# Before the first unit: only batch 0's odd half folded, on VectorE; its even half added up by DMAs during the first tile

## The chip, the cores and the metric

One core of one Trainium2 chip runs the whole program. The metric is the device time of one execution in microseconds; the time of a kernel is the median of its runs. Engines are called by the names of the profile: PE (TensorE), DVE (VectorE), ACT (ScalarE), POOL (GpSimd), and SP, the queue that issues most DMAs.

## The reference

```python
X = np.fft.fft(x, axis=1)            # x is (4, 3072, 256), float32
X = np.fft.fft(X, axis=2)
x = X.real.reshape(B * S, D)
h = x @ w_in                         # 256 -> 2048
x = np.maximum(0.01 * h, h) @ w_out  # 2048 -> 256
xk = mu_k * x + (1 - mu_k) * x_prev  # x_prev: one token earlier
xr = mu_r * x + (1 - mu_r) * x_prev
k = np.maximum(xk @ w_k, 0)          # 256 -> 1024
return sigmoid(xr @ w_r) * (k * k @ w_v)
```

Everything is float32, and the weights arrive as 64-bit floats.

## The kernel before

The real part of a Fourier transform over the sequence is a cosine transform of one mixture of the rows and a sine transform of another. Four rows of x (s, M-s, N-s, M+s, with N = 3072 and M = 1536) enter only through sums and differences; making these is the *fold*. Folded rows come in 6 groups of 128 per batch and give four classes: Pe and Qe (even frequencies; P cosine, Q sine) and Po and Qo (odd ones). A class is two PE products, `fft_a` with the first three groups and a first table, `fft_b` with the last three and a second table; ACT and DVE turn their results into a row of 768 values (`classes`). Tables a, b, a2, b2 serve the even classes, c, d, c2, d2 the odd ones. The transform over the 256 features is moved into the weights: `w_in_mm(q)` multiplies eighth q of w_in by a cosine and a sine table, `w_in_split` writes the result as two float32r parts, `w_in_row` takes one more small product from it. Weights are converted from 64-bit floats by ACT, DVE and POOL in steps (`w_in_parts`, and for w_out the three steps `wout[q][0..2]`): POOL makes the part `r`, for which PE's product or DVE's last step waits.

Feature 128 is its own column and is transformed apart: `c_fold` folds it, `c_a` and `c_b` multiply it (4 columns, one per batch), and its result goes to DRAM (`cd_o`, `cd_e`) and comes back broadcast as `cb`, which each unit adds.

After that each batch has three tiles of 512 columns, and a tile 16 *units* of 128 of the 2048 hidden features. In `step`, PE computes the P half of the next unit (`mm_a`, L548), the Q half of this one (`mm_b`, L560) and, two units later, the product with w_out (`outmm`, L571). DVE and ACT do `ev`, `g`, the leaky function and the split into `gh` and `gl`. `mm_b` adds onto the accumulator that DVE's `ev` has read, so PE waits for `ev`. In the first tile `boot(u)` also prepares the rest of w_in and w_out, and a loop table (`pe_u`, `qe_u`) says after which unit Pe and Qe of the batch are computed; beside it the next batch is folded by accumulating DMAs that POOL issues (`second`). The last 40% of the time is the second network.

The order on each engine is the order of the program text (the kernel is scheduled by hand), so an instruction that waits holds up all behind it on its engine. Before the first unit the text runs from L457 to the definition of `boot`. For batch 0 the fold (`full`) makes even and odd halves together, six DVE or POOL operations per group: groups 0, 1, 3 and 4 on DVE, 2 and 5 on POOL. Batch 0's four classes are float32 products (two PE passes each); later batches split into float32r parts (`fft_src`), nine one-pass products in place of three.

Of the kernel before, what the change touches and what calls it, by code (L numbers as in the profile page):

```python
# [78 lines left out]
def fft_mlp_kernel(ctx, tc, xa, xb, x7, x8, x87, tb, tbs, alt, ce, so, mu, w_in, w_out, w_k, w_v, w_r, out):  # L79
# [117 lines left out]
    def fold_ops(b):  # L197
        st, eo, o7s = {}, {}, []
        pm = fft.tile([P, 6, 2, 2, P], F32, tag="pm", bufs=1, name=f"pm{b}")
        if b == 0:  # L200
            plus, minus = pm[:, 0:3], pm[:, 3:6]
            plus, minus = (t.rearrange("p g i o n -> p (g i) o n") for t in (plus, minus))
            folded[b] = {"Pe": plus[:, :, 0], "Qe": minus[:, :, 1], "Po": minus[:, :, 0], "Qo": plus[:, :, 1]}
        else:
            for g in range(6):
                eo[g] = pm[:, g]
            folded[b] = pm, o7s

        def first(g, p=None):
            if b == 0:  # L210
                tag, bufs = ("yo", 2) if p is work else ("xl", 4)
                t = st[g] = p.tile([P, 2, 2, D], F32, tag=tag, bufs=bufs, name=f"xl{b}_{g}")
                Q.dma_start(t[:, 0], xa[b, g])
                Q.dma_start(t[:, 1], xb[b, g, :, :, 0:D])
            else:
                st[g] = fft.tile([P, 2, D], F32, tag="xl", bufs=2, name=f"xl{b}_{g}")
                Q.dma_start(eo[g][:, 0], xa[b, g, :, :, 0:P])
                Q.dma_start(st[g], xa[b, g])


        def second(g):
            E = eo[g][:, 0]
            G.dma_start(E, xa[b, g, :, :, P:D], accum_op=ALU.add)
            G.dma_start(st[g], xb[b, g, :, :, P:P + D], accum_op=ALU.add)
            G.dma_start(E, xb[b, g, :, :, 0:P], accum_op=ALU.add)
            G.dma_start(E, xb[b, g, :, :, P:D], accum_op=ALU.add)


        def full(g, E, tags):
            t = st[g].rearrange("p z o d -> p (z o) d")  # L230
            home = {"gh": mv, "gl": mv, "Qh": mv}
            e, o, eo[g] = (home.get(tag, work).tile([P, 4, P], F32, tag=tag, bufs=2, name=f"f{n}{g}")
                           for n, (tag, _) in zip("eoc", tags))
            eo[g] = eo[g].rearrange("p (z o) n -> p z o n", z=2)
            E.tensor_tensor(e, t[:, :, :P], t[:, :, P:], op=ALU.add)
            E.tensor_tensor(o, t[:, :, :P], t[:, :, P:], op=ALU.subtract)
            E.tensor_tensor(eo[g][:, 0], e[:, 0:2], e[:, 2:4], op=ALU.add)
            E.tensor_tensor(eo[g][:, 1], o[:, 0:2], o[:, 2:4], op=ALU.subtract)
            fin(g, 2, E)
            fin(g, 3, E)  # L240

        def fin(g, q, E=V):
            if q == 1:
                E.tensor_tensor(eo[g][:, 1], st[g][:, :, :P], st[g][:, :, P:], op=ALU.subtract)
            elif q == 2:
                E.tensor_tensor(plus[:, g], eo[g][:, :, 0], eo[g][:, :, 1], op=ALU.add)
            else:
                E.tensor_tensor(minus[:, g], eo[g][:, :, 0], eo[g][:, :, 1], op=ALU.subtract)
# [5 lines left out]
        def fold7(E=V):  # L254
# [6 lines left out]
            if b == 0:  # L261
                E.tensor_tensor(plus[0:1, 0, 1], o7[:, 0], o7[:, 1], op=ALU.subtract)
            else:
                o7s.append(o7)

        return first, second, full, fin, load7, fold7
# [8 lines left out]
    def fft_src(b, kind, h):  # L275
        pm, o7s = folded[b]
        i = 0 if kind[0] == "P" else 1
# [3 lines left out]
        s = pm[:, 3 * h:3 * h + 3, i]  # L281
        V.tensor_tensor(t, s[:, :, 0], s[:, :, 1], op=ALU.add if kind in ("Pe", "Qo") else ALU.subtract)
# [5 lines left out]
    def fft_mm(b, kind, h, ps, stop):  # L288
        t = tabs[KINDS[kind][h]]
        how = dict(skip_group_check=True) if h else {}  # L290
        if b == 0:
            src = folded[b][kind]
            terms = [(src[:, 3 * h + c], t[:, c]) for c in range(3)]
# [113 lines left out]
    def w_out_load(q, ahead=False):  # L407
        if q < 8:
            st = load_f64(w_out[q * 256:(q + 1) * 256].rearrange("(k p) d -> p k d", p=P), 2, D, ahead)
            s = slice(2 * q % HF, 2 * q % HF + 2)  # L410
            wout[q] = f64_hi_lo(uoh[2 * q // HF][:, s], uol[2 * q // HF][:, s], st, 2, D, *((mv, "gl") if q < 3 else (stage, "f")))


    def c_fold():
        c8 = mv.tile([P, 6, 2, 4], F32, tag="gh", bufs=2, name="c8")
        V.tensor_tensor(c8, x8t[:, :, 0:2], x8t[:, :, 2:4], op=ALU.add)
        V.tensor_tensor(c8p, c8[:, :, 0], c8[:, :, 1], op=ALU.add)
        V.tensor_tensor(c8m, c8[:, :, 0], c8[:, :, 1], op=ALU.subtract)
        V.memset(c87, 0.0)
        V.tensor_tensor(c87[0:1], x87t[:, 0], x87t[:, 1], op=ALU.add)  # L420

    def c_a(src, t0, extra):
        ps = ps_s.tile([P, 512], F32, tag="s", name="cps")
        for c in range(3):
            T.matmul(ps[:4, :JP], src[:, c], tabs[t0][:, c], start=(c == 0), stop=(c == 2 and not extra))
        if extra:
            T.matmul(ps[:4, :JP], c87, altt, start=False, stop=True)
        ev = work.tile([4, JP], F32, tag="fv", bufs=2, name="cev")
# [15 lines left out]
    pairs = [TORD[i:i + 2] for i in range(0, 8, 2)]  # L444
    later_tabs = 3 * TORD

    def next_pair():
        load_pair_tab(*pairs.pop(0))
# [52 lines left out]
    w_in_split(1)  # L501
    wout[0][0]()
    po = fft_a(0, "Po")
    ca = c_a(c8m, "c", False)
    w_in_row(1)
    w_in_parts(2)
    fft_b(0, "Po", *po)
    wout[0][1]()
    cs0 = c_b(c8m, "d", "o", *ca, "g")
    cur_c = load_c(0, 0)  # L510
    wout[1][0]()
    qo = fft_a(0, "Qo")
    wout[0][2]()
    next_pair()
    w_in_parts(3)
    wout[1][1]()
    fft_b(0, "Qo", *qo)
    next_pair()
    cur = split_tile(0, 0, "P") + split_tile(0, 0, "Q")
    w_in_mm(2)  # L520
# [260 lines left out]
    w_in_split(2)  # L781
    wout[1][2]()
    for b in range(B):

        pe_u, qe_u, f0, f1 = (2, 10, 13, 36) if b == 0 else (1, 4, 10, 36)
        po_u, qo_u = 37, 40
        done = 0
        for ti in range(NT):
# [3 lines left out]
            for u in range(NF):  # L792
# [292 lines left out]
```

## Time and profile before

| | |
|---|---|
| median of 3 runs (lowest to highest) | 1510.63 us (1509.85 to 1511.0) |
| the profiled execution's own time | 1511.04 us |
| its span in the trace | 1509.3 us |
| mean granted PE clock | 0.994 |
| PE busy in the span | 1479.3 us (98%) |
| DVE busy | 1032.8 us (68%) |
| ACT busy | 890.5 us (59%) |
| POOL busy | 168.2 us (11%) |

The span runs from the first to the last instruction; the execution's own time holds 1.74 us more around it. Times in rows count from the span's start. "Idle before" in brackets is how long an engine did nothing before that row, and what ended it.

### The profile page before, as it was taken

To read this page: it belongs to the slowest core of one execution; us is meant where nothing else is said; L and a number is where in the kernel's file an instruction comes from. 1 tells how busy PE (TensorE), PEld (TensorE's weight loads), DVE (VectorE), ACT (ScalarE), POOL (GpSimd) and SP (SyncE) were. 2 spreads that over 40 slices of the span, in tenths; PEclk is the share of its full clock that TensorE was granted. 3 is DMA by queue.
4 is the path that set the end of the run, shared out by engine and by line. 5 is a ranking of instruction groups with operands and counts; after the bars stand their busy time and mean duration, and the time that the engine had idled before them with its cause. 6 is when DMAs were issued, how large, how long until landed. Compare 5 with 4: busy or idle time off the path is not lost.

```text
span 1509.3 us, 17754 instructions
## 1 busy us (share of the span) xinstructions
PE 1479.3 (98%) x6506; PEld 1212.3 (80%) x6506; DVE 1032.8 (68%) x1426; ACT 890.5 (59%) x1469; POOL 168.2 (11%) x165
## 2 busy tenths in 40 slices
PE   5899999999999999999999999999999999999998
PEld 3677888888888888888888887888888888888887
DVE  8776667676767766666667775766667676766665
ACT  2565566656566656566566665656555656565554
POOL 4333401023101142010001000000000000000000
PEclk8999999999999999999999999999999999999999
DMA  7434723276213464132411102221212121211200
GB/s 252 140 95 110 119 56 129 85 195 103 35 67 123 164 123 92 14 122 99 137 43 36 56 1 84 84 71 56 71 56 84 43 84 44 83 63 63 70 29 28
DMA packets 97810, 128.71 MB, mean 85 GB/s; under 512 B 29190, under 2 KB 64775, under 8 KB 94650
## 3 DMA queue, kind: packets, MB, share of 16 engines
q1 hardware_dynamic: 74618, 87.29, 18.0%
q0 software_dynamic: 23104, 40.29, 11.7%
q8 instruction: 51, 0.84, 0.2%
q14 instruction: 37, 0.30, 0.1%
HBM read 99.67 MB, written 27.88 MB: 85 GB/s over the span
## 4 chain that ended last, share of the span: by engine, by line
PE 95%; DVE 1%; DMA 1%; ACT 0%; issue 0%; POOL 0%; ACTq 0%; DVEq 0%
PE o L571 34%; PE v L927 17%; PE kps L884 17%; PE ps L560 9%; PE ps L548 9%; PE rps L935 4%; PE wps L383 1%; PE dps L592 0%; DMA pm<-in_xa 0%; DMA xl<-in_xb 0%; PE cps L434 0%; PE f0Qe L299 0%; PE f0Pe L299 0%; PE f1Qe L299 0%; PE f2Qe L299 0%; DMA y<-yo 0%
## 5 line engine op out<-in xcount | busy, mean ns | idle before, releaser
L637 DVE SCALAR_TENSOR_TENSOR g<-ev,ps 128x512 f32<-128x512 f32 x192 | 131.7, 686 | 194.5 <-PE ps L560 194.4
L888 ACT ACTIVATE rl<-kps 128x512 f32<-128x512 f32 x190 | 113.9, 599 | 230.4 <-PE kps L884 227.0
L619 DVE TENSOR_TENSOR gl<-g,gh 128x1024 fp32r<-128x1024 f32 x192 | 239.5, 1248 | 1.4 <-ACT gh L104 1.4
L889 DVE SCALAR_TENSOR_TENSOR k<-kps,rl 128x512 f32<-128x512 f32 x190 | 131.6, 693 | 148.4 <-ACT rl L888 147.7
L104 ACT ACTIVATE gh<-g 128x1024 fp32r<-128x1024 f32 x192 | 202.8, 1056 | 51.1 <-PE o L571 50.0
L107 ACT ACTIVATE g<-ps 128x512 f32<-128x512 f32 x192 | 114.9, 598 | 163.6 <-DVE g L637 162.2
L571 PE MATMUL o<-gh,uoh 128*128 128x512 f32 x768 | 211.3, 389 | 0.0
L571 PE MATMUL o<-gh,uol 128*128 128x512 f32 x768 | 211.1, 389 | 0.0
L571 PE MATMUL o<-gl,uoh 128*128 128x512 f32 x768 | 211.1, 389 | 0.0
L571 PEld LDWEIGHTS o<-gh,uoh 128*128 128x128 f32 x768 | 144.2, 188 | 30.4
L571 PEld LDWEIGHTS o<-gl,uoh 128*128 128x128 f32 x768 | 144.2, 188 | 30.0
L571 PEld LDWEIGHTS o<-gh,uol 128*128 128x128 f32 x768 | 144.2, 188 | 29.9
L553 DVE SCALAR_TENSOR_TENSOR ev<-cb,w,ps 128x512 f32<-128x512 f32 x192 | 143.4, 747 | 2.6 <-PE ps L548 0.8
L111 DVE TENSOR_TENSOR k2l<-k,k2h 128x512 fp32r<-128x512 f32 x190 | 129.6, 682 | 0.5 <-ACT k2h L104 0.5
L927 PE MATMUL v<-k2h,wvh 128*128 128x512 f32 x382 | 121.7, 389 | 0.1
L927 PE MATMUL v<-k2l,wvh 128*128 128x512 f32 x382 | 121.5, 389 | 0.0
L927 PE MATMUL v<-k2h,wvl 128*128 128x512 f32 x382 | 121.5, 389 | 0.0
L107 ACT ACTIVATE g<-g 128x512 f32<-128x512 f32 x192 | 119.6, 623 | 0.0
L884 PE MATMUL kps<-mh,wkh 128*128 128x512 f32 x380 | 117.3, 390 | 1.5 <-ACT mh L104 0.8
L104 ACT ACTIVATE k2h<-k 128x512 fp32r<-128x512 f32 x190 | 118.4, 623 | 0.0
L884 PE MATMUL kps<-ml,wkh 128*128 128x512 f32 x380 | 117.2, 390 | 0.1
L884 PE MATMUL kps<-mh,wkl 128*128 128x512 f32 x380 | 117.0, 389 | 0.0
(392 smaller groups left out, 2280.4 us busy)
## 6 DMA issues: line engine op xcount, KB each, us to landing
y<-yo SPq DMA_DIRECT2D x24, 512.0 KB
xa<-y SPq DMA_DIRECT2D x24, 512.0 KB
out_dram<-o SPq DMA_DIRECT2D x23, 512.0 KB
tab_c<-in_tbs POOLq DMA_DIRECT2D x6, 1158.0 KB, 5.8
tab_d<-in_tbs POOLq DMA_DIRECT2D x6, 1158.0 KB, 5.5
tab_a<-in_tbs POOLq DMA_DIRECT2D x6, 1158.0 KB, 6.2
tab_b<-in_tbs POOLq DMA_DIRECT2D x6, 1158.0 KB, 5.5
xl<-in_xa SPq DMA_DIRECT2D x24, 256.0 KB
```

The costliest lines, as they stand in the source:

```text
L104: A.activation(o, i, ACTF.Copy)
L107: A.activation(o, i, ACTF.Prelu, alpha=0.01)
L111: V.tensor_tensor(lo, src, hi.bitcast(F32), op=ALU.subtract)
L548: T.matmul(x["ps"], l[:, f], r, start=(i == 0), stop=(i == 2))
L553: V.scalar_tensor_tensor(x["ev"], x["cb"], w128[:, u:u + 1], x["ps"], op0=ALU.mult, op1=ALU.add)
L560: T.matmul(x["ps"], l[:, f], r, start=False, stop=(i == 2), skip_group_check=True)
L571: T.matmul(po[s][h], w[:, u % HF, h * P:(h + 1) * P], g[:, s], start=(u == 0 and i == 0), stop=(u == NF - 1 and i == 2))
L619: V.tensor_tensor(gl, x["g"], x["gh"].bitcast(F32), op=ALU.subtract)
L637: V.scalar_tensor_tensor(g[:, 1], x["ev"], 2.0, x["ps"], op0=ALU.mult, op1=ALU.subtract)
L884: T.matmul(ps, w[:, k, sl], x[:, k], start=(i == 0), stop=(i == 5))
L889: V.scalar_tensor_tensor(k2, ps, 0.0, r, op0=ALU.max, op1=ALU.mult)
L927: T.matmul(vps[m], w[:, f, m * P:(m + 1) * P], x, start=(f == 0 and i == 0), stop=(f == NK - 1 and i == 2))
```

## The change

It redoes the part before the first unit. Batch 0's fold on the engines now makes only the odd half: `fold_odd`, four DVE operations per group, in place on the loaded rows. The even half (tile `pm`, both even classes) is one plain load by SP and three accumulating DMAs for each half of the groups, issued by POOL after units 1, 2 and 3 (`even0`). Pe and Qe of batch 0 then go the way of the later batches: `fft_src`, float32r tables (loaded by POOL), nine products for three; they move from units 2 and 10 to 5 and 8. The even part of feature 128 is split into float32r too. The host stores x as one array `xs` (the four rows beside one another, two of them with their halves swapped). Before the first unit the loads stand in another order, the odd products of feature 128 come first on PE, and w_in's eighths 1 and 2 move behind: eighth 1 between the halves of unit 0, eighth 2 and all later ones one `boot` pair later, and w_out's likewise. The fold of the later batches does the same sums from the new array, in pieces that are twice as long.

```diff
+        def even(h, k):
+            g = slice(3 * h, 3 * h + 3)
+            src = xs[b, g, :, k].rearrange("g p d -> p g d")
+            if k == 0:
+                Q.dma_start(pm[:, g, 0], src)
             else:
+                G.dma_start(pm[:, g, 0], src, accum_op=ALU.add)
...
+    def fold_odd(g, t):
+        h, c = divmod(g, 3)
+        if c == 0:
+            odd0.append(mv.tile([P, 3, 2, P], F32, tag="gh", bufs=2, name=f"odd{h}"))
+        o = odd0[h][:, c]
+        d = t.rearrange("p (z o) d -> p z o d", z=2)
+        V.tensor_tensor(d[:, :, 0], d[:, :, 0], d[:, :, 1], op=ALU.subtract)
+        V.tensor_tensor(t[:, 0], t[:, 0], t[:, 2], op=ALU.add)
+        V.tensor_tensor(o[:, 0], t[:, 0, :P], t[:, 0, P:], op=ALU.add)
+        V.tensor_tensor(o[:, 1], t[:, 0, :P], t[:, 0, P:], op=ALU.subtract)
...
     w_in_load(0)
+    Q.dma_start(x8t, x8)
+    load_plain("c")
     Q.dma_start(cet, ce)
     Q.dma_start(sot, so)
...
+    load_plain("d")
+    load7()
+    load_rows(0, 3)
+    load_plain("c2")
+    load_rows(3, 6)
+    load_plain("d2")
...
+    w_in_parts(0)
+    V.tensor_tensor(c8m, x8t[:, :, 0], x8t[:, :, 1], op=ALU.subtract)
...
+    fold7()
+    ca = c_a(c8m, "c", False)
+    w_in_mm(0)
+    cs0 = c_b(c8m, "d", "o", *ca, "g")
+    cur_c = load_c(0, 0)
+    w_in_load(1)
     w_out_load(0)
...
+    fold_odd(0, x0[0])
+    w_in_split(0)
+    fold_odd(1, x0[1])
     w_in_load(2, True)
     w_out_load(1, True)
+    fold_odd(2, x0[2])
+    w_in_row(0)
+    po = fft_a(0, "Po")
+    qo = fft_a(0, "Qo")
+    for g in range(3, 6):
+        fold_odd(g, x0[g])
+    even0(0, 0)
+    even0(1, 0)
     w_in_load(3)
+    fft_b(0, "Po", *po)
+    cur = split_tile(0, 0, "P")
+    w_in_parts(1)
     w_out_load(2)
...
+    fft_b(0, "Qo", *qo)
+    cur += split_tile(0, 0, "Q")
...
-    w_in_split(2)
-    wout[1][2]()
+    w_in_mm(1)
+    wout[0][0]()
+    w_in_split(1)
+    wout[0][1]()
+    w_in_parts(2)
...
-        pe_u, qe_u, f0, f1 = (2, 10, 13, 36) if b == 0 else (1, 4, 10, 36)
+        pe_u, qe_u, f0, f1 = (5, 8, 13, 36) if b == 0 else (1, 4, 10, 36)
...
+                if b == 0 and i < 2:
+                    next_tab()
+                if b == 0 and 0 < i < 4:
+                    even0(0, i)
+                    even0(1, i)
```

What DVE had in a row before, after the parts of w_in's first eighth (`fe`, `fo`, `fc` are steps of the old fold of groups 0 and 1, `xl` the loaded rows):

```order
L140 TENSOR_SCALAR h<-fv 128x512
L235 TENSOR_TENSOR fe_192<-xl_0_131 128x512
L236 TENSOR_TENSOR fo_193<-xl_0_131 128x512
L237 TENSOR_TENSOR fc_194<-fe_192 128x256
L238 TENSOR_TENSOR fc_194<-fo_193 128x256
L246 TENSOR_TENSOR pm_126<-fc_194 128x256
L248 TENSOR_TENSOR pm_126<-fc_194 128x256
L235 TENSOR_TENSOR fe_210<-xl_1_137 128x512
```

And now (`c8m` is feature 128, `cs` the end of its odd product, `x_0_138` group 0's rows, `odd` the folded result, L386 the split of w_in's first eighth):

```order
L140 TENSOR_SCALAR h<-fv 128x512
L481 TENSOR_TENSOR c8m<-x8t 128x24
L482 TENSOR_TENSOR c8p<-x8t 128x24
L483 TENSOR_TENSOR c8m<-c8m,c8p 128x24
L441 SCALAR_TENSOR_TENSOR cs<-cev,cps 4x384
L255 TENSOR_TENSOR x_0_138<-x_0_138 128x2x256
L256 TENSOR_TENSOR x_0_138<-x_0_138 128x256
L257 TENSOR_TENSOR odd_200<-x_0_138 128x128
L258 TENSOR_TENSOR odd_200<-x_0_138 128x128
L261 TENSOR_TENSOR odd_200<-x_0_136 1x128
L386 TENSOR_TENSOR wl_110<-wps_176,wh_109 128x2x256
```

The first fold operation stood directly behind the weight's steps; now three small operations and `cs` stand between, and each group has four operations, two of them of 128 columns.

POOL in the first units, before (`r` belongs to the weights, L144 its product, L158 a sum for w_out):

```order
L144 TENSOR_TENSOR r<-st,h 128x512
L158 TENSOR_TENSOR r<-r,fv 128x512
L144 TENSOR_TENSOR r<-st,h 128x512 x2
L158 TENSOR_TENSOR r<-r,fv 128x512
L144 TENSOR_TENSOR r<-st,h 128x512 x2
L158 TENSOR_TENSOR r<-r,fv 128x512
```

And now (`tab_a`, `tab_b` are float32r tables, each `pm ... x2` one accumulating step for the two halves of the groups):

```order
L144 TENSOR_TENSOR r<-st,h 128x512 x2
L189 DMA tab_a<-in_tbs 128x2316
L158 TENSOR_TENSOR r<-r,fv 128x512
L144 TENSOR_TENSOR r<-st,h 128x512
L189 DMA tab_b<-in_tbs 128x2316
L225 DMA pm_126<-in_xs 128x3x256 x2
L144 TENSOR_TENSOR r<-st,h 128x512
L225 DMA pm_126<-in_xs 128x3x256 x2
L158 TENSOR_TENSOR r<-r,fv 128x512
L144 TENSOR_TENSOR r<-st,h 128x512
L225 DMA pm_126<-in_xs 128x3x256 x2
L144 TENSOR_TENSOR r<-st,h 128x512
```

Between the weights' steps POOL now issues two tables and three pairs of accumulating DMAs; the second pair waits for the first to land, the third for the second.

## Rows read from the trace of the kernel before

**Rows 1.** Busy us of PE, PEld, DVE, ACT, POOL by stretch; PE clock, DMA share, GB/s.
```profile
0.00:46.00 46.00, 25.63 (x80) 15.41 (x80) 38.36 (x61) 15.55 (x30) 24.18 (x25) 0.89 0.65 222
46.00:60.00 14.00, 11.14 (x37) 8.52 (x38) 10.01 (x14) 6.63 (x14) 3.58 (x3) 0.76 0.67 251
60.00:100.00 40.00, 40.00 (x178) 29.95 (x177) 31.07 (x46) 25.10 (x44) 11.69 (x9) 1.00 0.22 69
148.00:250.00 102.00, 102.00 (x456) 84.73 (x455) 67.53 (x90) 61.66 (x99) 20.74 (x23) 1.00 0.43 90
```

**Rows 2.** Timeline of PE up to unit 2: start, duration, line, out<-in, count.
```profile
27.91 2.11 PE L425 MATMUL cps<-tab_c,c8m 128*4 128x386 f32 x6 [1.49 <-DVE c L419]
...
49.26 0.76 PE L560 MATMUL ps<-Qh,wh 128*128 128x512 f32 x1 [0.93 <-DVE ev L553]
...
58.51 0.50 PE L560 MATMUL ps<-Qh,wh 128*128 128x512 f32 x1 [0.84 <-DVE ev L553]
```

**Rows 3.** Timeline of DVE before the first unit.
```profile
6.37 0.43 DVE L140 TENSOR_SCALAR h<-fv 128x512 uint32<-128x512 uint32 x1
7.00 1.78 DVE L235 TENSOR_TENSOR fe<-xl 128x512 f32<-128x512 f32 x1 [0.20 <-DMA xl<-in_xb]
...
28.97 0.27 DVE L262 TENSOR_TENSOR pm<-x 1x128 f32<-1x128 f32 x1
29.18 0.67 DVE L235 TENSOR_TENSOR fe<-xl 128x512 f32<-128x512 f32 x1
...
30.38 0.40 DVE L237 TENSOR_TENSOR fc<-fe 128x256 f32<-128x256 f32 x1
...
37.81 0.54 DVE L438 SCALAR_TENSOR_TENSOR cs<-cev,cps 4x384 f32<-4x384 f32 x1 [0.75 <-ACT cs L104]
```

**Rows 4.** Stretches as in rows 1, at the lower granted clock.
```profile
18.80:24.10 5.30, 5.30 (x16) 4.23 (x17) 5.30 (x5) 0.00 (x0) 4.77 (x4) 0.50 0.99 367
...
49.30:54.70 5.40, 5.40 (x15) 4.46 (x16) 3.51 (x6) 2.98 (x6) 0.00 (x0) 0.50 0.76 295
```

**Rows 5.** DMA rate from 0 to 40 us, one number per us.
```profile
GB/s 0 27 225 372 331 344 337 298 316 378 352 278 307 229 296 302 243 286 287 278 359 391 399 406 396 412 398 399 389 309 125 33 0 0 0 8 0 0 0 0
```

**Rows 6.** DMA issues from 0 to 100 us: KB, us to landing.
```profile
cd_o<-cs POOLq DMA_DIRECT2D x1, 12.0 KB, 2.1
```

**Rows 7.** Timeline of POOL: one weight product; accumulating DMAs, an issue and the next.
```profile
62.20 1.31 POOL L144 TENSOR_TENSOR r<-st,h 128x512 fp32r<-128x512 f32 x1 [4.08 <-ACT gh L104]
...
135.20 1.07 POOL L225 DMA_DIRECT2D pm<-in_xb  x1 [1.43 <-DMA pm<-in_xa]
138.86 1.07 POOL L226 DMA_DIRECT2D pm<-in_xb  x1 [2.58 <-DMA pm<-in_xb]
...
185.03 1.08 POOL L224 DMA_DIRECT2D xl<-in_xb  x1 [4.64 <-DVE gl L619]
185.76 1.47 POOL L225 DMA_DIRECT2D pm<-in_xb  x1
190.65 1.08 POOL L226 DMA_DIRECT2D pm<-in_xb  x1 [3.42 <-DMA pm<-in_xb]
```

**Rows 8.** The page, DMA issues: KB each, median us to landing.
```profile
tab_b<-in_tbs POOLq DMA_DIRECT2D x6, 1158.0 KB, 5.5
```

**Rows 9.** Timeline of PE: one class half by either kind of product; weights in the first tile.
```profile
65.38 2.11 PE L299 MATMUL f0Pe<-tab_a,pm 128*128 128x386 f32 x6
67.33 0.81 PE L306 MATMUL f0Pe<-altt,e7p 128*128 128x386 f32 x2
...
78.14 0.17 PE L403 MATMUL wps<-one,wh 128*128 128x2 f32 x1
...
80.79 0.39 PE L560 MATMUL ps<-Qh,wh 128*128 128x512 f32 x1
...
289.70 0.51 PE L299 MATMUL f1Pe<-tab_a,sh1Pe 128*128 128x386 f32 x2
...
291.30 0.81 PE L306 MATMUL f1Pe<-altt,e7p 128*128 128x386 f32 x2
```

More of the change, by code (lines that the diff above doesn't have):

```diff
@@ L78, in fft_mlp_kernel @@
 @with_exitstack
-def fft_mlp_kernel(ctx, tc, xa, xb, x7, x8, x87, tb, tbs, alt, ce, so, mu, w_in, w_out, w_k, w_v, w_r, out):
+def fft_mlp_kernel(ctx, tc, xs, x7, x8, x87, tb, tbs, alt, ce, so, mu, w_in, w_out, w_k, w_v, w_r, out):
     nc = tc.nc
@@ L197, in fold_ops @@
     def fold_ops(b):
[L198 to L207, printed above, removed]
@@ L221, in second @@
[L221 to L240, printed above, removed]
@@ L242, in fin @@
[L242 to L248, printed above, removed]
+        st, o7s = {}, []
+        pm = fft.tile([P, 6, 2, D], F32, tag="pm", bufs=1, name=f"pm{b}")
+        folded[b] = pm, o7s
@@ new lines, in first, with second @@
+        def first(g):
+            st[g] = fft.tile([P, 2, D], F32, tag="xl", bufs=2, name=f"xl{b}_{g}")
+            Q.dma_start(pm[:, g, 0], xs[b, g, :, 0])
+            Q.dma_start(st[g], xs[b, g, :, 0:2])
+        def second(g):
+            E = pm[:, g, 0]
+            G.dma_start(E, xs[b, g, :, 1], accum_op=ALU.add)
+            G.dma_start(st[g], xs[b, g, :, 2:4], accum_op=ALU.add)
+            G.dma_start(E, xs[b, g, :, 2], accum_op=ALU.add)
+            G.dma_start(E, xs[b, g, :, 3], accum_op=ALU.add)
@@ L260, in fold7, with load_x0 @@
             E.tensor_tensor(e7p[0:1], e7[:, 0], e7[:, 1], op=ALU.add)
[L261 to L266, printed above, removed]
+            o7s.append(o7)
+        return first, second, fin, even, load7, fold7
+    def load_x0(g, p, tag, bufs):
+        t = p.tile([P, 4, D], F32, tag=tag, bufs=bufs, name=f"x0_{g}")
+        Q.dma_start(t, xs[0, g])
+        return t
+    odd0 = []
+    def fold_odd(g, t):
[8 more added lines that the diff above has]
+        V.tensor_tensor(o[:, 1], t[:, 0, :P], t[:, 0, P:], op=ALU.subtract)
+        if g == 0:
+            o7 = folded[0][1][0]
+            V.tensor_tensor(o[0:1, 1], o7[:, 0], o7[:, 1], op=ALU.subtract)
     folded, classes, srcs = {}, {}, {}
@@ L290, in fft_mm @@
         how = dict(skip_group_check=True) if h else {}
-        if b == 0:
-            src = folded[b][kind]
-            terms = [(src[:, 3 * h + c], t[:, c]) for c in range(3)]
+        if (b, kind[1]) == (0, "o"):
+            terms = [(odd0[h][:, c, 0 if kind[0] == "P" else 1], t[:, c]) for c in range(3)]
         else:
@@ L410, in w_out_load, with c_mm @@
             s = slice(2 * q % HF, 2 * q % HF + 2)
-            wout[q] = f64_hi_lo(uoh[2 * q // HF][:, s], uol[2 * q // HF][:, s], st, 2, D, *((mv, "gl") if q < 3 else (stage, "f")))
+            wout[q] = f64_hi_lo(uoh[2 * q // HF][:, s], uol[2 * q // HF][:, s], st, 2, D, *((mv, "gl") if q < 1 else (stage, "f")))
     def c_fold():
[L415 to L418, printed above, removed]
+        c8s = tuple(mv.tile([P, 6, 4], F32R, tag=n, bufs=2, name="c8" + n) for n in ("Qh", "Ql"))
+        V.tensor_tensor(x8t[:, :, 0:2], x8t[:, :, 0:2], x8t[:, :, 2:4], op=ALU.add)
+        V.tensor_tensor(c8p, x8t[:, :, 0], x8t[:, :, 1], op=ALU.add)
+        hi_lo(*c8s, c8p)
         V.memset(c87, 0.0)
         V.tensor_tensor(c87[0:1], x87t[:, 0], x87t[:, 1], op=ALU.add)
+        return c8s
+    def c_mm(ps, src, k, h, stop):
+        t = tabs[k]
+        how = dict(skip_group_check=True) if h else {}
+        if isinstance(src, tuple):
+            hi, lo = src
+            terms = [(w[:, 3 * h + c], t[:, i, c]) for c in range(3) for w, i in ((hi, 0), (hi, 1), (lo, 0))]
+        else:
+            terms = [(src[:, 3 * h + c], t[:, c]) for c in range(3)]
+        for n, (w, x) in enumerate(terms):
+            T.matmul(ps[:4, :JP], w, x, start=(h == 0 and n == 0), stop=(stop and n == len(terms) - 1), **how)
     def c_a(src, t0, extra):
         ps = ps_s.tile([P, 512], F32, tag="s", name="cps")
-        for c in range(3):
-            T.matmul(ps[:4, :JP], src[:, c], tabs[t0][:, c], start=(c == 0), stop=(c == 2 and not extra))
+        c_mm(ps, src, t0, 0, not extra)
         if extra:
             T.matmul(ps[:4, :JP], c87, altt, start=False, stop=True)
-        ev = work.tile([4, JP], F32, tag="fv", bufs=2, name="cev")
+        ev = fft.tile([4, JP], F32, tag="x7", bufs=1, name="cev") if extra else work.tile([4, JP], F32, tag="fv", bufs=2, name="cev")
         act_copy(ev, ps[:4, :JP])
@@ L432, in c_b @@
     def c_b(src, t1, par, ps, ev, tag):
-        for c in range(3):
-            T.matmul(ps[:4, :JP], src[:, 3 + c], tabs[t1][:, c], start=False, stop=(c == 2), skip_group_check=True)
+        c_mm(ps, src, t1, 1, True)
         cs = work.tile([4, CP], F32, tag=tag, bufs=2, name="cs")
@@ L443, in fft_mlp_kernel @@
     tabs = {}
[L444 to L448, printed above, removed]
+    later_tabs = TORD[4:] + 3 * TORD
     def next_tab():
@@ L500, in fft_mlp_kernel @@
     uol.append(wo.tile([P, HF, D], F32R, name="uol1"))
[L501 to L520, printed above, removed]
     def boot(u):
@@ L804, in fft_mlp_kernel @@
                     boot(u)
-                if b == 0 and i == 6:
-                    half = c_a(c8p, "a", True)
+                if b == 0 and i < 2:
[3 more added lines that the diff above has]
+                    even0(1, i)
+                if b == 0 and i == 2:
+                    c8s = c_fold()
+                if b == 0 and i == 5:
+                    chalf = c_a(c8s, "a", True)
                 if b == 0 and i == 7:
-                    c_b(c8p, "b", "e", *half, "yo")
-                    next_tab()
+                    c_b(c8s, "b", "e", *chalf, "yo")
                 for kb, kind, k_u in ((b, "Pe", pe_u), (b, "Qe", qe_u), (b + 1, "Po", po_u), (b + 1, "Qo", qo_u)):
@@ L836, in fft_mlp_kernel @@
                     while f0 <= i and done < 6 and done * (f1 - f0) < 6 * (i - f0 + 1):
-                        fin(done, 1)
+                        fin(done)
                         if done < 5:
```

102 lines of the change are left out of this document (39 added, 63 removed).

## The prediction

> **What bounds the kernel now.** I read busy time by stretch first [rows 1]. From 60 to 100 us PE is busy all the time, and from 148 to 250 as well; DVE has room there (31.1 of 40 us). There a change counts only by the PE work that it removes or the waits that it adds. Before 46 us it is the other way round: DVE is busy 38.4 of 46 us and PE 25.6, so what ends last is DVE's list of folds and weight steps; from 46 to 60 PE stands idle 2.9 us more. So the change is worth how much earlier PE gets into the units, less the work that moves behind that point, less new waits in the first tile. In the timeline of PE the reader finds two marks [rows 2]: the Q half of unit 0 at 49.26 and that of unit 2 at 58.51, each behind DVE's `ev`. The timeline of DVE [rows 3] shows the prices: 0.67 us for 128x512 and 0.40 for 128x256 where POOL is quiet, 1.78 for the first fold while POOL multiplies; the nearest row to 128x128 is one of 1x128, 0.27. The granted clock [rows 4]: at 0.50, the 1.2 GHz level, through 5.3 and 5.4 us of unbroken PE work that followed a mostly idle stretch.
>
> **Until DVE can fold.** DVE is through with the first weight steps at 6.8 [rows 3], and three tiny operations take it to 7.4. Next in its row is `cs`, the end of feature 128's odd product. It needs the products `c_a` and `c_b` and, as in the row of before, ACT's copy. PE starts at 7.4: table c and all ahead of it are 1.17 MB, which the DMA rate [rows 5] sums to at 5.6 us; some 0.8 us to landing (an estimate: the first rows of x, 1.31 MB by the same sum at 6.1, let DVE go at 7.0) makes 6.4. At full clock `c_a` takes 2.1 us [rows 2], w_in's product about 2.3 (the stretch from 78.14 to 80.79 [rows 9], less 0.4 for four small ones), `c_b` 2.1. At half clock for the first 5.3 us, as in rows 4: `c_a` to 11.7, 1 us of the next at half, the rest of it to 14.6, `c_b` to 16.7. ACT's copy 0.5 and `cs` 0.54: **DVE folds from 17.8.** If the upper level came only after `c_b`, 21.9.
>
> **The folds.** Four operations per group: 0.67 + 0.40 + 0.27 + 0.27 = 1.6; six groups 9.7, one small row 0.27, the split of the first eighth 0.67: done at 28.4. By the price under POOL, 1.78 in place of 0.67, they would take 7 us more; POOL only issues one DMA meanwhile, so I take the lower. The rows don't bind: group 5 ends at 5.76 MB, by the same sum 20.8, landed at 21.6, needed at 26.7. SP's queue now stands behind `cd_o` (2.1 us to landing [rows 6], so until about 20.7) before it loads w_in's eighth 1; that lands at about 25 and is needed at 30.6.
>
> **To unit 0.** From 28.4: Po's last product 0.7, ACT 0.5, DVE 0.55, ACT's Ph 0.6, Pl 0.67: 31.4. Then three steps of eighth 1 (1.55), Qo's second part 0.55, ACT's row and Qh 1.4, Ql 0.67, `ev` 0.75: **the Q half of unit 0 at 36.5, 12.8 us earlier.** PE's Qo product and eighth 1 lie beside this.
>
> **To unit 2.** DVE now has w_out's first steps, the split of eighth 1 and the steps of eighth 2 ahead of unit 0's `g`: 1.55 + 0.67 + 1.55 = 3.8 us to 40.3. POOL's two products and a sum (1.31 each [rows 7]) end at 41.9, so eighth 2 is through at 43.6; unit 1's Q half and unit 2's P half 1.4, `ev` 0.75: 46.2. Before it was 58.51: **-12.3.**
>
> **Given back and saved behind.** One eighth with its small products is now behind that mark: 78.14 to 80.79 [rows 9], +2.65. Six halves (two each of Pe, Qe, feature 128) go from three float32 products (65.38 to 67.33, 1.95) to nine float32r ones (289.70 to 291.30, 1.60): -0.35 each, -2.1 together. Without new waits: -11.75. DVE's added `fft_src` and splits (about 1.1 us, four times) have room where it is busy 78% [rows 1]. Later batches' longer DMA pieces lie where PE is never idle: nothing.
>
> **POOL's queue in the first tile.** This is where the change adds a wait. POOL issues table b at about 51.2 (behind the weight product of eighth 3); it lands 5.5 later [rows 8], and the accumulating calls, 384 KB each, stand in line behind it. Step 2 of a half may only be issued when step 1 has landed, and step 3 after step 2; behind the second step wait w_out's sum and the product of eighth 4. The rows give a price [rows 7]: 256 and 128 KB issued at 185.03 and 185.76 had landed at 190.65, 5.6 us; the small `cd_o` takes 2.1, so moving 384 KB took 3.5. Those went in pieces of 1 KB and 512 bytes, these all in 1 KB, so 2.6 if pieces count; with weight loads in between I take **3.0 per call in line.** Ends for the range: 1.0 (the best rate of rows 5, 400 GB/s) and 11 (three times the 3.66 from 135.20 to 138.86). At 3.0: step 1 lands at 59.7 and 62.7, POOL is free at 63.8, eighth 4's product is done at 66.4, and PE, due there at 62.5, loses 3.9. Step 3's first half lands at 71.7; Pe's first half, needing another 1.6 us of DVE and ACT, is due at 74.1 by then: no second wait. **+4.**
> The Trainium skill ("DMA: Bandwidth & Descriptors", the anatomy of one DMA on the GpSimd path) fits 2.0 us plus the bytes at 436 GB/s, 2.9 us for 384 KB. The row shows 5.6 for as many bytes, and the measurement decides; by the page the +4 would be 0 and the time that of the first rival.
>
> **Clock.** Before, 5.4 us of the first units ran at half [rows 4], which cost 2.7. My schedule has none of it; PE is about half busy from 32 to 45, so I expect part of it: between 0 and 2.7, **+1** taken.
>
> **Sum:** -12.3 + 2.65 - 2.1 + 4 + 1 = -6.75. The profiled execution took 1511.04 (span 1509.3), 0.4 above the median 1510.63; against the median this is **1504**.
>
> **The rivals.**
> - *The accumulations are quick enough.* At 1.0 per call step 1 lands at 57.7 and 58.7, eighth 4's `r` is done at 62.4 and PE never waits: 1500, or 1499 if the clock costs nothing. For it: 1 KB pieces. Against: the 5.6 us. Chance 0.2.
> - *The clock stays low until `c_b` is through.* DVE's folds and all after them come 4.1 us later: 1508. For it: feature 128's product stands first, on a PE that has done nothing. Against: both stretches of rows 4 were followed by the full clock. Chance 0.12.
> - *Slower: DVE held at `fft_src`.* Place: DVE's first even source of Pe, after unit 4, which waits for step 3 of the first half; all of DVE's unit work stands behind it. Five calls in line after table b make its landing 56.7 + 5 times the price. Pe's first product would be due at 70.2 without any wait and needs the landing plus 1.6. The loss reaches the 10.75 that is gained (clock counted) at a landing of 79.3, so from **4.5 us per call**; at 6 it is 18 and the time 1518. For it: 3.66 us for a 128 KB step, and weight loads on the same DMA engines; against: the 5.6 for three times that. Chance 0.1; between 3.5 and 4.5 the time lies at 1505 to 1510, chance 0.13.
>
> **The numbers.** The forecast keeps 0.45. The range reaches from the first rival to the middle of the last in-between case, **1498.5 to 1510**; beyond it lie the slower rival and some of the edges. A difference of 0.2% (3 us) is about the least that a measurement of this kernel can tell from none. Faster than 1507.6: the forecast 0.45, the first rival 0.2, and over half of the two middle cases: 0.79. Within 0.2%: 0.12. Slower: 0.09.
>
> **What would show it.** `cs` on DVE at about 17.3 after some 10 us of idle time, ended by ACT or PE; fold operations of 0.67, 0.40, 0.27, 0.27; Q halves of units 0 and 2 near 36.5 and 46.2. In the first tile: POOL idle before its second and third accumulating pairs, ended by DMA; PE waiting for POOL's `r` at the product of eighth 4 by some 4 us, and not for `sl` of Pe. Halves of Pe and Qe at 1.6 us. If PE waits at Pe instead, the third rival holds; if unit 0 starts after 41, the second; if PE is fully busy from 47 on, the first. It would all be wrong if the folds cost near 1.78 an operation, or if rows arrived after 26.7.

## The result and the profile after

The changed kernel takes **1519.38 us** (median of 4 runs, 1517.61 to 1520.07) where the kernel before takes 1510.82 (1509.85 to 1511.05) on the same chip: ratio 1.0056, interval 1.0039 to 1.0074. It is **8.6 us slower**; 1504 was predicted and the range ended at 1510. The span is 1517.8 us.

Busy time by stretch, after (the columns of [rows 1]):

```profile
0.00:46.00 46.00, 28.61 (x84) 15.67 (x85) 25.95 (x56) 15.38 (x29) 9.40 (x13) 0.91 0.68 242
46.00:60.00 14.00, 13.16 (x54) 10.52 (x53) 11.22 (x19) 7.96 (x15) 7.88 (x8) 0.82 0.44 150
60.00:100.00 40.00, 30.73 (x128) 23.19 (x127) 24.63 (x38) 20.45 (x37) 16.15 (x13) 0.90 0.73 175
100.00:148.00 48.00, 45.49 (x214) 37.63 (x213) 38.62 (x57) 27.27 (x51) 19.45 (x19) 0.98 0.53 148
148.00:250.00 102.00, 102.00 (x453) 83.94 (x452) 66.99 (x86) 61.94 (x99) 16.53 (x21) 1.00 0.38 84
```

The reader compares the third row with that of before: PE was busy 40.00 of 40 us there and is now busy 30.73, while DVE has fallen from 31.07 to 24.63 and POOL has risen from 11.69 to 16.15. Before 46 us it went as meant: DVE's 38.36 are 25.95 now. So the front got cheaper, and the first tile behind it lost more than that. From 148 us on PE is fully busy in both.

Timeline of PE, after (start, duration, engine, line, operation, out<-in; in brackets the idle time before and what ended it; L545 is `mm_a`, L557 `mm_b`, L376 and L378 w_in's product):

```profile
8.45 4.02 PE L425 MATMUL cps<-tab_c,c8m 128*4 128x386 f32 x6 [8.45 <-DVE c8m L483]
...
38.21 0.47 PE L557 MATMUL ps<-Qh,wh 128*128 128x512 f32 x1 [0.27 <-DVE ev L550]
...
51.34 0.51 PE L557 MATMUL ps<-Qh,wh 128*128 128x512 f32 x1 [0.84 <-DVE ev L550]
...
73.44 0.79 PE L378 MATMUL wps<-r,cer 128*128 128x256 f32 x2 [5.13 <-POOL r L144]
...
83.73 0.62 PE L292 MATMUL f0Pe<-tab_a,sh0Pe 128*128 128x386 f32 x2
...
88.35 0.50 PE L545 MATMUL ps<-Ph,wh 128*128 128x512 f32 x1 [1.41 <-ACT g L107]
...
98.12 0.50 PE L545 MATMUL ps<-Ph,wh 128*128 128x512 f32 x1 [2.31 <-ACT g L107]
...
124.72 1.13 PE L376 MATMUL wps<-fv,cet 128*128 128x256 f32 x4 [1.25 <-ACT g L107]
```

The first three rows answer to [rows 2]: the Q half of unit 0 is 11.05 us earlier than before, that of unit 2 7.17. Of the other five, which are new, one is a wait for POOL's weight part `r`, three are waits of PE for ACT's `g`, and one is Pe's first product, at 83.73, which waits for nothing.

Timeline of POOL, after (L225 are the accumulating calls):

```profile
55.94 0.57 POOL L189 DMA_DIRECT2D tab_b<-in_tbs  x1
56.51 2.67 POOL L225 DMA_DIRECT2D pm<-in_xs  x2
59.75 1.31 POOL L144 TENSOR_TENSOR r<-st,h 128x512 f32<-128x512 f32 x1 [0.57 <-PE ps L545]
65.92 1.28 POOL L225 DMA_DIRECT2D pm<-in_xs  x1 [4.86 <-DMA pm<-in_xs]
69.56 1.30 POOL L225 DMA_DIRECT2D pm<-in_xs  x1 [2.36 <-DMA pm<-in_xs]
70.37 1.78 POOL L158 TENSOR_TENSOR r<-r,fv 128x512 f32<-128x512 f32 x1
71.59 1.80 POOL L144 TENSOR_TENSOR r<-st,h 128x512 fp32r<-128x512 f32 x1
72.82 1.81 POOL L225 DMA_DIRECT2D pm<-in_xs  x1
```

POOL stands still twice, 4.86 and 2.36 us, until the halves of step 1 have landed; the `r` that PE waits for at 73.44 stands behind both. Timeline of DVE, after:

```profile
18.01 0.54 DVE L441 SCALAR_TENSOR_TENSOR cs<-cev,cps 4x384 f32<-4x384 f32 x1 [9.62 <-ACT cs L104]
18.48 0.67 DVE L255 TENSOR_TENSOR x<-x 128x512 f32<-128x512 f32 x1
19.19 0.43 DVE L256 TENSOR_TENSOR x<-x 128x256 f32<-128x256 f32 x1
19.65 0.29 DVE L257 TENSOR_TENSOR odd<-x 128x128 f32<-128x128 f32 x1
...
41.34 1.63 DVE L137 SCALAR_TENSOR_TENSOR fv<-st,h 128x512 uint32<-128x512 uint32 x1
...
80.15 0.56 DVE L276 TENSOR_TENSOR t0Pe<-pm 128x384 f32<-128x384 f32 x1 [4.58 <-DMA pm<-in_xs]
```

Stretches at a lower granted clock, after (columns as above; the answer to [rows 4]):

```profile
45.00:50.00 5.00, 4.99 (x14) 4.02 (x14) 2.74 (x5) 2.34 (x6) 2.28 (x3) 0.50 0.01 3
70.00:75.00 5.00, 1.56 (x5) 1.38 (x6) 2.79 (x3) 0.00 (x0) 4.68 (x5) 0.66 0.74 105
75.00:80.00 5.00, 5.00 (x18) 4.04 (x17) 0.54 (x2) 0.00 (x0) 3.91 (x3) 0.66 1.02 211
...
95.00:100.00 5.00, 2.69 (x10) 1.87 (x10) 2.66 (x5) 4.00 (x7) 2.89 (x2) 0.89 0.37 105
100.00:105.00 5.00, 5.00 (x21) 3.48 (x20) 3.13 (x5) 0.73 (x2) 1.31 (x1) 0.77 0.00 0
```

**Where the lead goes.** Start of a unit's Q half, us, in the kernels of this study (from PE's timelines, one execution of each; the last column is unit 0 of the second tile):

| kernel | unit 0 | unit 4 | unit 5 | unit 8 | unit 12 | next tile |
|---|---|---|---|---|---|---|
| before | 49.26 | 73.73 | 80.79 | 100.74 | 123.95 | 143.51 |
| changed | 38.21 | 62.61 | 76.17 | 106.43 | 132.72 | 152.07 |
| no accumulation | 37.48 | 62.74 | 69.60 | 98.80 | 125.09 | 144.44 |
| feature 128 early | 38.90 | 64.26 | 79.34 | 98.12 | 126.55 | 145.90 |
| neither wait | 38.17 | 64.67 | 73.15 | 91.92 | 118.61 | 137.97 |
| even classes later | 38.19 | 62.59 | 75.99 | 98.13 | 123.50 | 147.35 |
| spaced | 37.75 | 63.42 | 70.28 | 91.33 | 116.70 | 139.50 |
| early start alone | 31.88 | 55.80 | 69.10 | 99.25 | 125.68 | 145.03 |
| spaced, both edits | 32.13 | 56.09 | 62.99 | 84.03 | 109.39 | 129.98 |

The changed kernel is 11.1 us ahead at units 0 and 4, 4.6 at unit 5, 5.7 behind at unit 8 and 8.6 behind at the second tile, the whole difference. (At unit 2 it is 7.2 ahead. Pe's two halves stand between units 2 and 4 before and between 5 and 8 now, 3.9 and 3.6 us of PE: they lift the lead at unit 4 and lower it at unit 8. From unit 4 to 5 both kernels do the same work.)

### The profile page after: what moved, and what is told of

The parts are those of the page before. It is cut to its first block, busy times and chain, and to the rows that moved or that the text cites. A ratio compares the mean times of both kernels' runs of the same rounds, so it can differ in the third digit from the quotient of the medians.

```text
span 1517.8 us, 17787 instructions
## 1 busy us (share of the span) xinstructions
PE 1482.3 (98%) x6524; PEld 1216.0 (80%) x6524; DVE 1027.4 (68%) x1434; ACT 892.6 (59%) x1474; POOL 149.9 (10%) x166
## 4 chain that ended last, share of the span: by engine, by line
PE 94%; DVE 2%; ACT 1%; DMA 1%; issue 1%; POOL 0%; POOLq 0%; ACTq 0%; DVEq 0%
PE o L568 33%; PE v L931 17%; PE kps L888 17%; PE ps L545 8%; PE ps L557 8%; PE rps L939 4%; DMA pm<-in_xs 1%; PE dps L589 0%; PE wps L376 0%; PE f0Po L292 0%; DVE fv L137 0%; POOL r L144 0%; PE f0Pe L292 0%; PE wps L378 0%; PE f1Qe L292 0%
```

## The experiments

Two theories. **A, the accumulating chain:** POOL cannot issue a step before the last has landed, and a call takes some 3 us in line; PE loses the wait for `r` and what the clock does behind it. **B, accumulators:** four are in `ps_s`. In the changed kernel feature 128's product (`cps`, units 5 to 7) and Pe (`f0Pe`, units 5 to 7) hold two at once, w_in's product a third, so the next unit's P half has to wait until ACT has read the last one (the factors of a P half are long there, so what `g` sets free for it is the accumulator). Before, Pe stood in units 2 and 3, feature 128 in 6 and 7, and they did not meet. The experiments take each away alone, then both; a fifth accumulator was not tried. All ratios are to the kernel before, run beside them.

**No accumulation.** Leaves out three of the four rows of batch 0's even half.

```diff
-                if b == 0 and 0 < i < 4:
-                    even0(0, i)
-                    even0(1, i)
```

> Leaves out the three accumulating DMAs of batch 0's even half (two of its classes are then made of one row in four; every instruction on the engines stays). The theory that POOL's queue costs the time (product r of eighth 4 held behind the second accumulating pair, DVE held at the first source of Pe): PE's wait of 5.1 us for r and the low clock after it (2.4) go, DVE no longer waits 4.6 us, and nothing of the wait of the P half of unit 7 for ACT's g is left: 1508 us or less. The rival, that feature 128 and Pe hold two of the four accumulators at once: the 5.1 and 2.4 go, but PE still waits for ACT's g at the P halves of units 7 and 8 by 1 to 2 us each (1.41 and 2.31 now) with the low clock after them: 1510 to 1513 us.

Measured: 1512.12 us (ratio 1.0010, 1.0000 to 1.0019), 7.3 under the changed kernel. PE no longer waits for this `r`, and the clock stays at 1.00 from 70 to 80 us. The two terms come to about as much: 5.13 of wait, and 0.34 of the 6.56 us that PE was busy there, 2.2. DVE's first source of Pe, at 71.03, waits for nothing. But the waits for ACT's `g` are as long as in the changed kernel (PE's timeline):

```profile
80.72 0.50 PE L545 MATMUL ps<-Ph,wh 128*128 128x512 f32 x1 [1.41 <-ACT g L107]
...
90.50 0.50 PE L545 MATMUL ps<-Ph,wh 128*128 128x512 f32 x1 [2.33 <-ACT g L107]
...
117.09 1.13 PE L376 MATMUL wps<-fv,cet 128*128 128x256 f32 x4 [1.25 <-ACT g L107]
```

So A is worth 7 us, and these waits are not its echo, nor that of DVE's wait at Pe.

**Feature 128 early.** Its products in units 3 and 4, away from Pe.

```diff
-                if b == 0 and i == 5:
+                if b == 0 and i == 3:
                     chalf = c_a(c8s, "a", True)
-                if b == 0 and i == 7:
+                if b == 0 and i == 4:
```

> Moves only the even products of feature 128, from units 5 and 7 to units 3 and 4, so that their accumulator is free before Pe takes one. POOL's-queue theory: the same time as the change, 1518 to 1520 us, and the P halves of units 7 and 8 still wait for ACT, since ACT and DVE are late from their wait at the first source of Pe. Accumulator theory: those two waits (3.7 us together) and the low clock behind them (1.7) go, the wait for r of eighth 4 (5.1) stays: 1513 to 1515 us.

Measured: 1510.99 us (1.0006, 0.9997 to 1.0015) (the profiled execution: 1513.39). PE's waits between unit 2 and the second tile (waited for: us in total, times, longest):

```profile
PE wps L378 <- POOL r L144: 3.8, 1, 3.8
PE ps L557 <- DVE ev L550: 2.1, 2, 1.3
PE wps L376 <- ACT g L107: 1.8, 1, 1.8
```

No P half waits for ACT, and the wait for `r` is shorter, since feature 128's products run ahead of it. The third row is w_in's last product, in unit 10 (1.25 in the changed kernel): there Qe holds an accumulator, which this edit does not move. DVE still stands idle for 4.16 us before 80.05, but for ACT's part of feature 128's row; its first source of Pe follows at 80.52 without a wait.

**Even classes later.** The other way to part them: Pe and Qe after units 7 and 10.

```diff
-        pe_u, qe_u, f0, f1 = (5, 8, 13, 36) if b == 0 else (1, 4, 10, 36)
+        pe_u, qe_u, f0, f1 = (7, 10, 13, 36) if b == 0 else (1, 4, 10, 36)
```

> Pe and Qe of batch 0 at units 7 and 10 in place of 5 and 8, all else as in the change. Both theories: the wait for r of eighth 4 stays at about 5 us, since POOL's order up to there is untouched. POOL's-queue theory: DVE's wait of 4.6 us at the first source of Pe goes (its data land by 81 us and it is asked for two units later), and with it most of what followed: 1513 us. Accumulator theory: feature 128 and Pe overlap in one unit only, so the waits of P halves for ACT go: 1513 to 1514 us. If neither wait mattered, 1519.

Measured: 1513.88 us (1.0021, 1.0010 to 1.0032). PE's waits in the same stretch:

```profile
PE wps L378 <- POOL r L144: 5.0, 1, 5.0
PE ps L557 <- DVE ev L550: 3.5, 2, 2.7
```

The P halves' waits for ACT are gone here too, whichever of the two moves, and that of w_in's last product as well, since Qe now comes behind it; the wait for `r` stays. That is what B says.

**Neither wait.** No accumulation (three of four rows left out) and feature 128 early, both diffs above.

> The changed kernel without the accumulating steps (three of the four rows of batch 0's even half are left out) and with feature 128's products in units 3 and 4. Alone the first edit gave 1512.1 us and the second 1511.0. If POOL's chain and the shortage of accumulators are two separate costs, of some 7 and 5 us, the gains add for the most part: 1504 to 1507 us, with PE neither waiting for POOL's r nor for ACT's g in units 5 to 8. If they are one cost seen twice (POOL's lateness makes the units that run short), the time stays at 1510 to 1512 us.

Measured: 1505.19 us (0.9960, 0.9946 to 0.9974), 14.2 under the changed kernel where the two gains add to 15.7 (7.3 and 8.4). A and B are two costs. From unit 2's Q half to the second tile the clock is now 1.00 and PE busy 83.75 us, where it was 83.78 before.

**Plain loads.** The later steps overwrite, so three of four rows are left out, but the calls, bytes and queue stay.

```diff
-                G.dma_start(pm[:, g, 0], src, accum_op=ALU.add)
+                G.dma_start(pm[:, g, 0], src)
```

> The changed kernel with its six later steps of batch 0's even half written as plain loads, on the same queue and of the same 384 KB, so that each step overwrites the sums instead of adding to them (the output leaves out three of the four rows of the even half). If adding at the target is what made a call cost 3.3 to 3.6 us in line, a pair now lands within some 3 to 4 us of its issue (384 KB at the 400 GB/s that the loads of the first 18 us reach is 1 us), POOL's r is no longer late by 5 us, DVE does not wait for the even half at unit 5, and the time falls to that of the kernel without these steps, about 1512 us. If it is the queue or the bytes and not the adding, the landings stay at 7 to 8 us, PE's wait for POOL's r stays near 5 us and the time stays at 1517 to 1520 us.

Measured: 1512.41 us (1.0014, 1.0005 to 1.0023), the time without these calls (the profiled execution: 1514.34). POOL's timeline, where the second step is issued:

```profile
64.19 0.79 POOL L225 DMA_DIRECT2D pm<-in_xs  x1 [3.19 <-DMA pm<-in_xs]
65.30 0.77 POOL L225 DMA_DIRECT2D pm<-in_xs  x1 [0.31 <-DMA pm<-in_xs]
```

The two halves land 1.11 us apart; in the changed kernel it was 3.64 (65.92 and 69.56). PE's wait for `r` is 1.01 us. POOL's queue from 56 to 82 us moves the same bytes in a third of the packets (packets, MB, share of the 16 engines): first plain,

```profile
q0 software_dynamic: 816, 3.55, 37.9%
```

then accumulating, in the changed kernel:

```profile
q0 software_dynamic: 2543, 3.55, 72.7%
```

The median landing fell from 7.4 to 5.1 us; only the second step's calls came near the 3 to 4 expected (3.6 and 4.2, where the accumulating ones took 5.3 and 4.9). The first two stand behind table b in line. Whether the adding itself or the smaller packets that come with it is what costs was not tried.

**Spaced.** Even classes later, and the accumulating steps two units apart with the tables between them.

```diff
-                if b == 0 and i < 2:
+                if b == 0 and i in (0, 2, 4):
+                    even0(0, i // 2 + 1)
+                    even0(1, i // 2 + 1)
+                if b == 0 and i in (1, 3):
                     next_tab()
-                if b == 0 and 0 < i < 4:
-                    even0(0, i)
-                    even0(1, i)
```

> Pe and Qe at units 7 and 10 as in the run before, and POOL's issues spread: accumulating steps after units 0, 2 and 4, the float32r tables after units 1 and 3, so that no step waits in POOL's queue for the one before. POOL's-queue theory: no wait of PE for r longer than 1 us in units 3 to 6, no wait of DVE for the accumulated data; the gain of the earlier start (7 us at unit 2, 11 at unit 4) is kept but for the weight work that moved: 1502 to 1506 us. If the accumulating DMAs cost by their load on the DMA engines and not by their place in the queue: the wait moves to the loads of weights and the time stays over 1510 us.

Measured: **1506.97 us (0.9979, 0.9970 to 0.9988)**, faster than before, and 6.9 under even classes later, from which it differs by the order of POOL's issues alone: about what A was worth. PE's waits between unit 2 and the second tile, and the stretch that lost 9.3 us:

```profile
PE ps L557 <- DVE ev L550: 4.2, 4, 2.3
PE wps L378 <- POOL r L144: 0.6, 1, 0.6
```

```profile
60.00:100.00 40.00, 39.47 (x190) 31.17 (x189) 34.33 (x53) 25.50 (x46) 20.12 (x17) 1.00 0.78 213
```

The accumulating calls land no sooner (median 7.7 us), though the two of a step land only 2.0 to 2.2 us apart; POOL simply no longer comes to one before the last has landed. What is left in ACT's timeline is the fetch of Qe's class row from memory:

```profile
127.18 0.42 ACT L104 ACTIVATE Qh<-c0Qe 128x256 fp32r<-128x256 f32 x1 [3.37 <-DMA c0Qe<-cd_e]
```

**Spaced, with the folds ahead.** The class row no longer holds DVE up before the first unit.

```diff
-    cs0 = c_b(c8m, "d", "o", *ca, "g")
-    cur_c = load_c(0, 0)
     w_in_load(1)
     w_out_load(0)
-    Q.dma_start(x87t, x87)
-    Q.dma_start(altt[0:1], alt)
     fold_odd(0, x0[0])
-    w_in_split(0)
     fold_odd(1, x0[1])
     w_in_load(2, True)
     w_out_load(1, True)
     fold_odd(2, x0[2])
-    w_in_row(0)
+    cs0 = c_b(c8m, "d", "o", *ca, "g")
+    cur_c = load_c(0, 0)
+    Q.dma_start(x87t, x87)
+    Q.dma_start(altt[0:1], alt)
+    w_in_split(0)
     po = fft_a(0, "Po")
     qo = fft_a(0, "Qo")
+    w_in_row(0)
```

> The kernel with spaced steps and later classes, and besides the order ahead of the first unit changed: the folds of groups 0 to 2 stand ahead of the class row's eviction on VectorE, and the loads that wait for nothing stand ahead of the class row's on the load queue. VectorE waited 9.3 us there (8.4 to 17.7 us) for the class row, with the rows of x landing meanwhile. If that wait is what sets the start, PE's first odd half begins near 17.2 us instead of 21.75, unit 0's Q half near 32 instead of 37.75, and the time falls by 4 to 6 us, to 1501 to 1503 us. If something else is late by then (w_in's loads, POOL's chain, the clock), the units from the fifth on stand where they stood, and the time stays within 1.5 us of 1507 us.

Measured: 1500.70 us (0.9937, 0.9923 to 0.9950), 6.3 less. DVE's first fold and PE's first odd half:

```profile
9.85 0.93 DVE L255 TENSOR_TENSOR x<-x 128x512 f32<-128x512 f32 x1 [1.55 <-DMA x<-in_xs]
```

```profile
16.20 2.20 PE L292 MATMUL f0Po<-tab_c,odd 128*128 128x384 f32 x6
...
31.07 0.47 PE L557 MATMUL ps<-Qh,wh 128*128 128x512 f32 x1 [0.25 <-DVE ev L550]
```

**Spaced, with the class row copied.** ACT copies it from the tile where it was made.

```diff
-            if b == 0 and par == "o":
-                act_copy(y[0:1, :CW[par]], cs0[0:1, :CW[par]])
+            if b == 0:
+                act_copy(y[0:1, :CW[par]], cs[par][0:1, :CW[par]])
...
-                    c_b(c8s, "b", "e", *chalf, "yo")
+                    cs["e"] = c_b(c8s, "b", "e", *chalf, "yo")
```

> The kernel with spaced steps and later classes, with the even class row of feature 128 taken from the tile where it was made, by an ACT copy, and not fetched from memory behind fft_b of Qe. PE's wait of 2.28 us for ev in unit 12 goes back over ACT's wait of 3.37 us for that transfer. If it sets the end, the time falls by 1.5 to 2.5 us, to about 1504.5 to 1505.5 us; if ACT was late there for other reasons (its own evictions), the wait stays over 1.5 us and the time at 1507 us.

Measured: 1504.36 us (0.9961, 0.9948 to 0.9975), 2.6 less; PE's wait of 2.28 us for `ev` ahead of unit 14's Q half, behind that fetch, is 0.96.

**Both edits on the spaced kernel.**

> Both edits on the kernel with spaced steps. If the two waits are apart in the program and both set the end, the gains add: 5.5 to 8.5 us under 1507 us, about 1498.5 to 1501.5 us. If the earlier start is used up before unit 12, it is the time of the class row's edit alone, near 1505 us.

Measured: **1497.51 us (0.9920, 0.9906 to 0.9933)**, the best of all, 12.9 us under the kernel before and 9.5 under the spaced one; the parts add to 8.9. From 60 to 100 us PE is never idle:

```profile
60.00:100.00 40.00, 40.00 (x196) 32.23 (x195) 34.69 (x49) 24.39 (x44) 18.26 (x16) 1.00 0.66 180
```

**Early start alone.** The folds ahead on the changed kernel itself, everything else as there; the diff is that of the spaced kernel with the folds ahead.

> The changed kernel with only the order ahead of the first unit altered, as in the spaced kernel with that order, which gained 6 us by it; the accumulating steps stay bunched behind units 1 to 3. If the lead of the first units is lost to POOL's chain and the accumulators wherever the units start, the losses stay the same size and move forward with the units: 1512 to 1515 us, 5 to 7 us under the changed kernel. If the chain's end is set by the transfers (tables, w_in, w_out, x) and not by the units, the earlier start meets it as a longer wait and the time stays at 1517 to 1520 us.

Measured: 1512.72 us (1.0012, 1.0003 to 1.0022), 6.7 under the changed kernel. The losses move with the units and keep their size:

```profile
31.88 0.47 PE L557 MATMUL ps<-Qh,wh 128*128 128x512 f32 x1 [0.26 <-DVE ev L550]
...
66.38 0.79 PE L378 MATMUL wps<-r,cer 128*128 128x256 f32 x2 [4.89 <-POOL r L144]
...
81.18 0.50 PE L545 MATMUL ps<-Ph,wh 128*128 128x512 f32 x1 [1.63 <-ACT g L107]
...
90.96 0.70 PE L545 MATMUL ps<-Ph,wh 128*128 128x512 f32 x1 [2.33 <-ACT g L107]
```

So what the start gives carries through; it is the order in the first tile that loses, wherever that tile begins.

## Why the prediction was wrong

The prediction's own ledger, against the two traces. From unit 2's Q half to the second tile PE was busy 83.78 us and idle 1.22 before; after, busy 88.94 and idle 11.79.

| term | predicted | measured |
|---|---|---|
| start of unit 2 | -12.3 | -7.17 |
| one eighth given back, float32r | +0.55 | with the clock, +5.16 busy |
| clock | +1 | (in the rows above) |
| new waits | +4 | +10.57 |
| sum | -6.75 | +8.56 |

**Until DVE can fold: right.** `c_a` took 4.02 us and `c_b` 2.11, as at half and at full clock in the sum (read off the durations: the profile's clock column has 1.00 there throughout); folds from 18.48 where 17.8 stood. The rival with the clock low until `c_b` fell.

**The folds and unit 0: nearly right.** 0.67, 0.43, 0.29, 0.28; done at 29.1 for 28.4, and unit 0 at 38.21 for 36.5. That rival was to show itself by unit 0 "after 41".

**To unit 2: mis-sized.** Unit 0 to 2 took 13.1 us, not 9.7. DVE's two longer steps of eighth 2 took 0.92 and 1.63 (the row at 41.34) while POOL multiplied, where 0.43 and 0.69 are the quiet price; the sum had charged POOL's price nowhere behind the folds. And eighth 2's product fell into the 5 us at clock 0.50. (Three sums are themselves off by up to 0.5 us: 21.9 adds up to 21.4, 36.5 to 36.3, and 46.2 to 45.8. They would move the forecast by 0.6 us at most.)

**Given back: right in size.** Pe's second half takes 1.59 us, from 104.84 to 106.43 in PE's timeline, where 1.60 was taken. In the spaced kernel with both edits, where the clock is 1.00 from unit 2's Q half to the second tile, PE is busy 84.33 us there: 0.55 over before, the sum's figure (with neither wait it is 83.75, so the reading is no finer than that).

**POOL's queue: the wait was right, "no second wait" was the step that failed.** The prediction put PE's wait at the product of eighth 4, by 3.9 us; it is there, with 5.13. The price of 3.0 us per call held for the two that count: table b, issued at 55.94, took 7.6 us to land where 5.5 was taken, and 6.0 behind that, at 69.56, POOL had both halves of step 1, the second 3.64 after the first. By the Trainium skill ("DMA: Bandwidth & Descriptors", the anatomy of one DMA on the GpSimd path) a call of 384 KB would take 2.9 us from issue to landing, an estimate by its fit. Here the accumulating calls took 4.9 us and more and the plain ones 3.6 and more, with others in line, and the measurement decides.

But behind it came what the prediction never counted. The change moves Pe to unit 5, beside feature 128's product, and the prediction put the accumulators at nothing. PE's waits on ACT's `g` and `w` come to 5.2 us: 1.41, 0.26 and 2.31 in units 6 and 7, beside feature 128 and Pe, and 1.25 in unit 10, beside Qe. The Trainium skill ("Perfetto Trace Analysis", Identifying Performance Opportunities) says that a gap that recurs on the engine that should be full can mean too little SBUF or PSUM for the next tile; the two kernels that part the holders agree, with no P half waiting for ACT. Of the +10.57, then, 5.13 is A and 5.2 is B; the rest is DVE's `ev`.

**The slower rival: the right sign by another mechanism.** DVE was held at `fft_src` (4.58 us at 80.15), past the landing of 79.3 from which that rival was to decide, though a call cost 3.0 us in line and not 4.5: table b came 6.8 us later than the sum had it (63.5 for 56.7). But PE, held up for `r` before, came to Pe's product only at 83.73 and waited for nothing there, where that rival had it wait. Without accumulation DVE is not held, and PE's waits for ACT are the same.

**Clock: mis-sized.** +1 was taken for the first units; the 5 us from 45 on cost 2.5, about as much as before [rows 4], and lie within the -7.17. Behind the two waits it cost again: 2.2 us from 70 to 80, which came with the wait for `r` and went with it, and from 95 to 105, behind the wait of 2.31, 0.11 of 2.69 us and 0.23 of 5.00, 1.45 together. Beside the 0.55 given back that leaves some 1 us of the +5.16; cut to where the clock is 0.50 (PE busy 4.96 us from 71.6 to 78.4, and all of 98.9 to 102.3) the two cost 2.5 and 1.7, and 0.4 is left. With neither wait the clock is 1.00 there throughout.

Feature 128 early gained 8.4 us by the medians and 6.2 between the profiled executions (1519.58 and 1513.39). The 6.2 are there in the rows: 4.9 of idle time (4.0 of the waits for ACT, 1.4 of the wait for `r`, less 0.6 that w_in's last product waits longer), 0.8 of busy time, and 0.45 by which unit 2 starts earlier. The other 2.2 lie between executions of one kernel, and what differs there stays open.

## What to carry to other kernels

When work is moved into a busy stretch, list for each unit there what it holds (accumulators, buffers) and not only what it costs: two holders that never met before can make the next unit wait for the last reader. A chain of transfers that one engine must issue in turn is to be spaced by its time to landing, so that the engine never comes to a link before the last one is in; here that took away all but 0.6 us of the wait for the same transfers. And of an early start, first look for what stands at the head of the engine's line without need: 6.3 us lay there.

## What the runs showed of the hardware that was not expected

- Of two accumulating DMAs of 384 KB in line the second landed 3.64 us after the first, of two plain ones at the same place 1.11, on the same queue; 2543 packets against 816 for the same 3.55 MB. The price of an accumulating one is no constant: in the spaced kernel the two of a step landed 2.0 to 2.2 us apart.
- Spacing the accumulating steps did not make them land sooner (median 7.7 us against 7.4), and still took away all but 0.6 us of the wait behind them.
- The granted clock was 0.66 from 70 to 80 us, in a stretch with a PE wait of 5.13 us in it, and 1.00 there without accumulation, with plain loads and with spaced steps, where that wait is gone or down to 1 us: the wait cost 5.1 and the clock 2.2 on top.
